# Streaming-window attention and an affine ResMLP on one core: the same tasks in another written-out order, with other engines and buffers

## The chip, the cores and the metric

The kernel runs on one core of one Trainium2 chip. The core has five engines, each with an instruction queue of its own that is worked through strictly in order: PE (TensorE, the matmul array), DVE (VectorE), ACT (ScalarE), POOL (GpSimd) and SP (SyncE, which here only issues DMAs). ACT and POOL can issue DMAs too. Engines wait for each other by semaphores; an instruction that waits holds up everything behind it on its engine.

The metric is the device time of one execution in microseconds (us), the median of several runs. One execution was profiled as well, and everything said of single instructions is from that one.

## The reference, cut to what matters

```python
# q, k, v: [4, 8, 768, 64]; n_sink 4, window 128
scores = scale * q @ k.transpose(0, 1, 3, 2)
keep   = (pos_k < n_sink) | ((0 <= pos_q - pos_k) & (pos_q - pos_k < window))
a      = softmax(where(keep, scores, -1e9))
x      = (a @ v)  as [4, 768, 512]

a1  = alpha1 * x + beta1
tok = einsum("ts,bsd->btd", w_tok, a1)        # w_tok: [768, 768]
u   = x + lam * tok
a2  = alpha2 * u + beta2
ch  = relu(a2 @ w_ch1) @ w_ch2                # 512 -> 2048 -> 512
out = u + lam * ch
```

## The kernel before

The four batches go one after another through the same stages, and the stages of neighbouring batches are interleaved. A row block is 128 of the 768 positions, so a batch has six; heads are taken in pairs, or in two groups (G) of four.

*Loading.* `load_qk` (L412) loads one pair of heads of q or k. For the pairs 1 to 3 of batch 0 POOL issues a DMA that casts to fp16 on the way; the rest come as fp32 on SP's or ACT's queue and are cast by an engine (`trans`, L505; the casts and copies are done in a helper and have its lines, L168 on ACT and L170 on DVE and POOL). `load_v0` (L441) loads v of batch 0, `load_wtok` (L458) w_tok, `load_w` (L468) a part of the second weight (512 KB, `wst_w`), `load_w1` (L474) the first weight by POOL. `gate` (L481) is a tiny DMA on SP that waits for a part of the first weight; loads behind it on SP start no sooner. Semaphores of a queue's DMAs are used in turn, eight of them, so a DMA waits for the landing of the one eight before it.

*Attention.* `trans` transposes q and k by matmuls with an identity (tp, L532 and L535) into a PSUM bank, and an engine copies them out (qkT). Scores are matmuls with qkT (S, L645, and L709 in `scores_by_pair`), ACT takes the exponential (E, L667, L714), masks are put on, and `pv` (L735) multiplies by v (cast to vfs) and divides by the sum.

*The ResMLP.* alpha1 and beta1 arrive as rows la_b and lb_b (`la1_b` and `lb1_b` in the code) in four partitions; `fold_rows` (L1317) multiplies them by lam (lam_r) and spreads them by a shuffle (L1319, L1321). In batch 0, xh is x times la_b. `cast_wtok` (L830) casts a row block of w_tok (wt, L842 or L844), transposes it (wT, L837) and copies it out (wtokT). `tok` (L868) multiplies wtokT and xh, and adds the result to x; u is cast, transposed (uTp, L921), and `mlp1` (L952) gives h, which ACT or DVE turns into hT (relu). `prod` (L1163) and `mlp2` (L1260) multiply by the second weight (P, ch).

*What sets the order.* All of this is written as some 1230 tasks, by `Plan.add`, which has nothing to say about when they run. Three tables do: `ORDER` lists the task numbers in the order in which their instructions are written into the queues; digit i of `ENGINES` is the engine of task i (0 to 4: ACT, DVE, PE, POOL, SP); `HOMES` gives the number of the buffer or PSUM bank that each buffer of a task lives in. `IDLES` names five tasks ahead of which dummy matmuls (`idle`, L161) are written to keep PE running, with the PSUM bank that they write and their count: 67 ahead of task 46 in bank 0, 25 ahead of task 90 in bank 1, and three smaller blocks. `emit` puts it together:

```python
for i in order:
    t = self.tasks[i]
    e = (ACT, DVE, PE, POOL, SP)[int(engines[i])]
    idle = fills.get(i)
    if idle:
        self.fill[1](self.pools["d"][0].tile(
            [128, 512], FP32, tag=f"d_{idle[0]}", bufs=1, name=f"idle{t.i}"), idle[1])
    ...
    t.fn(e)
```

Semaphores follow from that: an instruction waits for what it reads, and for the last user of the buffer that it writes.

Of the kernel before, what the change touches and what calls it, by code (L numbers as in the profile page):

```python
# [80 lines left out]
def kernel(  # L81
# [129 lines left out]
    for r in range(NR):  # L211
# [18 lines left out]
        6, 7, 0, 26, 1, 10, 5, 2, 9, 11, 45, 18, 8, 19, 48, 3, 22, 15, 46, 4, 49, 12,  # L230
        50, 14, 17, 47, 13, 16, 90, 43, 103, 39, 41, 91, 28, 72, 104, 95, 53, 54, 63,
        51, 42, 73, 52, 21, 44, 74, 20, 96, 109, 100, 40, 107, 110, 65, 24, 68, 108, 92,
        69, 55, 61, 56, 93, 97, 101, 98, 59, 30, 94, 102, 111, 23, 99, 62, 113, 57, 114,
        25, 112, 116, 60, 105, 115, 58, 27, 128, 64, 106, 117, 31, 131, 135, 29, 129,
        125, 132, 138, 66, 130, 179, 78, 126, 122, 178, 140, 118, 139, 123, 197, 127,
        136, 119, 137, 32, 70, 146, 120, 141, 133, 33, 84, 79, 134, 124, 144, 147, 80,
        85, 71, 150, 121, 86, 142, 75, 67, 154, 143, 151, 76, 148, 158, 155, 145, 152,
        77, 87, 166, 156, 159, 81, 162, 167, 160, 88, 163, 82, 168, 89, 213, 157, 164,
        34, 35, 83, 209, 153, 217, 149, 214, 218, 210, 229, 219, 211, 215, 212, 226,
        165, 216, 36, 230, 185, 220, 161, 177, 223, 222, 176, 232, 221, 224, 204, 225,  # L240
        175, 227, 257, 169, 237, 233, 279, 238, 199, 234, 171, 258, 273, 280, 231, 186,
        259, 228, 274, 182, 277, 172, 260, 241, 278, 174, 246, 200, 295, 170, 248, 247,
        291, 296, 37, 181, 187, 243, 293, 292, 242, 289, 198, 294, 384, 267, 188, 290,
        281, 268, 173, 271, 349, 282, 180, 285, 272, 358, 301, 351, 286, 378, 303, 189,
        203, 297, 302, 192, 304, 249, 366, 190, 379, 298, 250, 287, 369, 380, 385, 205,
        288, 283, 191, 375, 386, 367, 265, 284, 368, 352, 370, 363, 376, 266, 253, 381,
        377, 371, 299, 254, 372, 615, 364, 206, 300, 382, 201, 365, 373, 275, 374, 383,
        357, 261, 276, 183, 387, 408, 262, 614, 263, 409, 202, 269, 184, 411, 410, 395,
        264, 239, 621, 617, 412, 397, 240, 270, 388, 400, 396, 235, 616, 196, 244, 398,
        401, 255, 245, 236, 390, 256, 193, 359, 389, 251, 399, 207, 311, 195, 252, 391,  # L250
        424, 426, 393, 335, 392, 360, 425, 636, 312, 194, 427, 208, 336, 394, 648, 428,
        413, 634, 419, 414, 622, 404, 420, 337, 405, 429, 402, 415, 313, 422, 416, 421,
        361, 441, 305, 403, 442, 638, 423, 626, 406, 314, 640, 619, 437, 315, 430, 443,
        316, 435, 431, 641, 338, 436, 362, 618, 433, 306, 438, 649, 341, 317, 432, 407,
        444, 637, 644, 307, 345, 439, 339, 620, 318, 445, 434, 628, 635, 450, 642, 308,
        451, 340, 440, 452, 639, 446, 453, 417, 319, 447, 645, 323, 418, 320, 309, 448,
        643, 658, 321, 324, 623, 449, 322, 329, 625, 659, 454, 646, 325, 347, 647, 330,
        455, 343, 326, 344, 353, 355, 464, 456, 465, 348, 466, 460, 650, 457, 467, 327,
        458, 331, 629, 461, 459, 462, 653, 632, 651, 463, 656, 332, 654, 356, 472, 627,
        652, 333, 342, 310, 38, 655, 660, 624, 480, 473, 468, 469, 470, 474, 885, 665,  # L260
        471, 476, 481, 475, 482, 488, 477, 350, 483, 492, 489, 478, 630, 490, 657, 493,
        479, 514, 491, 516, 328, 515, 882, 663, 518, 880, 517, 879, 498, 666, 661, 664,
        502, 499, 354, 508, 519, 512, 346, 509, 662, 678, 513, 671, 484, 679, 676, 486,
        503, 504, 487, 485, 677, 506, 877, 672, 680, 548, 507, 526, 505, 549, 334, 674,
        631, 522, 527, 907, 546, 681, 523, 633, 903, 528, 547, 534, 878, 529, 890, 675,
# [12 lines left out]
        986, 773, 752, 913, 886, 761, 919, 774, 604, 767, 918, 598, 762, 763, 768, 777,
        764, 779, 920, 923, 780, 987, 988, 989, 990, 914, 991, 992, 993, 755, 915, 778,
        608, 756, 926, 930, 735, 609, 924, 927, 931, 925, 753, 736, 781, 737, 893, 928,  # L280
        775, 782, 738, 892, 929, 934, 754, 932, 769, 610, 935, 941, 770, 819, 776, 894,
        942, 939, 820, 821, 940, 937, 936, 823, 749, 822, 748, 945, 824, 938, 747, 827,
        933, 948, 950, 750, 943, 952, 951, 825, 953, 787, 828, 944, 807, 788, 797, 826,
        808, 949, 946, 829, 954, 798, 801, 830, 791, 802, 947, 956, 792, 783, 957, 994,
        995, 996, 997, 961, 789, 784, 962, 958, 963, 964, 955, 790, 785, 959, 811, 965,
        805, 812, 786, 795, 806, 960, 967, 796, 799, 793, 968, 970, 966, 972, 794, 813,
        969, 971, 815, 973, 814, 809, 800, 974, 816, 803, 810, 976, 804, 978, 837, 975,
        979, 977, 835, 838, 980, 841, 836, 818, 839, 843, 842, 840, 981, 845, 844, 998,
        846, 817, 1002, 832, 831, 1006, 999, 1003, 1000, 1014, 1007, 1004, 1001, 833,
        1008, 1018, 1005, 834, 1022, 1015, 1009, 1019, 1016, 847, 1020, 1023, 1017, 851,  # L290
        848, 1021, 850, 855, 1010, 1024, 1012, 1011, 862, 1025, 1013, 852, 849, 856,
        868, 854, 858, 1050, 859, 1051, 863, 857, 869, 1026, 864, 1034, 860, 1082, 1028,
        1027, 871, 861, 1029, 870, 1030, 865, 853, 1031, 874, 872, 1032, 866, 1035, 873,
        1066, 867, 875, 1052, 1054, 876, 1033, 1053, 1056, 1055, 1038, 1058, 1083, 1036,
        1039, 1057, 1037, 1040, 1063, 1059, 1042, 1041, 1064, 1067, 1084, 1060, 1047,
        1043, 1085, 1070, 1048, 1072, 1061, 1071, 1074, 1045, 1049, 1062, 1068, 1065,
        1044, 1073, 1046, 1069, 1086, 1088, 1075, 1087, 1079, 1090, 1098, 1076, 1080,
        1114, 1099, 1077, 1115, 1089, 1081, 1078, 1095, 1100, 1091, 1116, 1096, 1130,
        1092, 1117, 1093, 1101, 1131, 1102, 1104, 1094, 1097, 1103, 1118, 1106, 1132,
        1162, 1119, 1134, 1133, 1120, 1111, 1135, 1122, 1136, 1112, 1146, 1138, 1127,  # L300
        1164, 1147, 1105, 1121, 1107, 1113, 1152, 1143, 1123, 1154, 1150, 1128, 1137,
# [1181 lines left out]
```

## Time and profile before

| | us |
|---|---|
| median of 3 runs | 250.66 (250.23 to 251.75) |
| span of the profiled execution, first to last instruction | 248.4 |
| PE busy | 242.9 (98%) |
| DVE busy | 208.0 (84%) |
| ACT busy | 136.1 (55%) |
| POOL busy | 126.0 (51%) |

The page gives the profiled execution's span, and not its time by the clock of the runs; the median of the runs is 2.3 us above that span. Names in the profile have their buffer numbers left out (la_b, qkT, S). A row of a group or of a timeline reads: line, engine, operation, output and inputs, shapes, count; in a timeline the first two numbers are start and duration in us, and a bracket at the end is the idle time of the engine just before it, with what ended it. PEld is PE's weight load, which runs beside its matmuls.

### The profile page before, as it was taken

Reading aid. Unit: us, or ns where it says so; the run is one execution under the profiler, and the core shown is the slowest. Engines: PE = TensorE matmul, PEld = TensorE weight load, DVE = VectorE, ACT = ScalarE, POOL = GpSimd, SP = SyncE. Lnnn points to the kernel's source line nnn. Section 1 sums busy time; section 2 is a strip of 40 time slices with the busy share of each in tenths; the row PEclk is TensorE's granted clock in tenths of the full one; section 3 lists DMA queues with packets and bytes.
Section 4 is the critical chain, followed back from the end, with each engine's and each line's share of the span. In section 5 each row is a group of like instructions: output and inputs, shape, how many; then the busy total and the mean of one; then the engine's idle time right before and its main releaser. Section 6 shows DMA issues by size and latency. Waiting matters only on the chain.

```text
span 248.4 us, 5583 instructions
## 1 busy us (share of the span) xinstructions
PE 242.9 (98%) x2151; PEld 159.2 (64%) x2151; DVE 208.0 (84%) x437; ACT 136.1 (55%) x229; POOL 126.0 (51%) x139
## 2 busy tenths in 40 slices
PE   8899999999999999999999999999999999999994
PEld 8654645676555544565677577568668477667883
DVE  6797987677697896798789998979798999899873
ACT  2399935688987124687833353666771234766000
POOL 8808733968866647413874012053746036556060
PEclk9999999999999999999999999999999999999999
DMA  6999999999999998899469445611000055200114
GB/s 207 210 247 297 248 211 304 355 362 287 219 196 210 254 179 178 180 247 200 106 131 203 85 84 161 170 21 45 3 0 3 4 101 186 93 0 3 65 42 150
DMA packets 86562, 38.80 MB, mean 156 GB/s; under 512 B 73588, under 2 KB 81276, under 8 KB 86536
## 3 DMA queue, kind: packets, MB, share of 16 engines
q1 hardware_dynamic: 67408, 29.11, 50.3%
q10 hardware_dynamic: 15384, 6.06, 10.4%
q0 software_dynamic: 3744, 3.28, 8.2%
q8 instruction: 17, 0.28, 0.5%
q14 instruction: 9, 0.07, 0.1%
HBM read 29.91 MB, written 6.29 MB: 146 GB/s over the span
## 4 chain that ended last, share of the span: by engine, by line
PE 90%; ACT 4%; DVE 3%; issue 2%; DVEq 0%; ACTq 0%
PE h L960 24%; PE P L1199 22%; PE tok L880 12%; PE ch L1269 8%; PE hA L1041 4%; PE pv L746 4%; PE S L645 4%; PE idle L161 2%; PE hE L1041 2%; PE tp L535 1%; ACT wt L842 1%; ACT E L667 1%; PE hB L1041 1%; DVE qkT L170 1%; PE tp L532 1%
## 5 line engine op out<-in xcount | busy, mean ns | idle before, releaser
L960 PE MATMUL h<-uT,w1f 128*128 128x384 f16 x384 | 68.0, 326 | 0.1
L960 PEld LDWEIGHTS <-w1f 128*128 128x128 f16 x384 | 35.9, 98 | 24.0 <-issue 2.0
L1199 PEld LDWEIGHTS <-hT 128*128 128x128 f16 x408 | 39.4, 98 | 6.6 <-DVE hT L1142 0.3
L667 ACT ACTIVATE E<-S 128x1024 f16<-128x1024 f32 (+1 forms) x39 | 38.0, 1002 | 7.0 <-PE S L645 5.4
L966 ACT ACTIVATE hT<-h 128x384 f16<-128x384 f32 x58 | 27.9, 492 | 21.5 <-PE h L960 17.9
L790 POOL TENSOR_TENSOR tm<-x,la_b 128x512 f32<-128x512 f32 x18 | 24.7, 1371 | 21.9 <-DVE xh L793 12.0
L880 PE MATMUL tok<-xh,wtokT 128*128 128x512 f16 x144 | 32.8, 379 | 0.0
L968 DVE TENSOR_SCALAR hT<-h 128x384 f16<-128x384 f32 x38 | 20.4, 553 | 8.1 <-PE h L960 7.7
L168 ACT CAST u<-x 128x512 f16<-128x512 f32 x17 | 10.4, 618 | 29.2 <-DVE x L887 28.0
L1199 PE MATMUL P<-w2f,hT 128*128 128x256 f16 x216 | 26.4, 273 | 0.0
L1212 DVE TENSOR_TENSOR x<-x,P 128x256 f32<-128x256 f32 x45 | 18.0, 415 | 7.2 <-PE P L1199 6.9
L880 PEld LDWEIGHTS <-wtokT 128*128 128x128 f16 x144 | 13.8, 98 | 15.2 <-issue 0.2
L1199 PE MATMUL P<-w2s,hT 128*128 128x256 f16 x192 | 22.9, 273 | 0.0
L1269 PE MATMUL ch<-w2f,hT 128*128 128x512 f16 x96 | 22.7, 379 | 0.0
L772 DVE TENSOR_TENSOR x<-pv,rec 128x256 f32<-128x256 f32 x48 | 20.4, 425 | 1.7
L168 ACT CAST n<-nat 128x768 f16<-128x768 f32 x20 | 16.2, 830 | 8.1 <-DMA out_dram<-x 4.8
L746 PEld LDWEIGHTS <-E 128*128 128x128 f16 x328 | 15.2, 97 | 4.9 <-issue 1.1
L170 POOL CAST u<-x 128x512 f16<-128x512 f32 x7 | 4.6, 663 | 26.1 <-DVE x L887 16.9
L746 PE MATMUL pv<-vfs,E 128*128 128x65 f16 x328 | 17.7, 194 | 0.0
L887 DVE TENSOR_TENSOR x<-x,tok 128x512 f32<-128x512 f32 x24 | 15.9, 681 | 1.8 <-PE tok L880 1.5
L607 POOL TENSOR_SCALAR_AFFINE_SELECT E<-E 128x512 f16<-128x512 f16 x12 | 8.6, 740 | 16.9 <-ACT E L667 16.9
L170 POOL CAST vfs<-vnat 128x512 f16<-128x512 f32 x18 | 13.9, 778 | 5.1 <-PE pv L746 4.2
(161 smaller groups left out, 432.4 us busy)
## 6 DMA issues: line engine op xcount, KB each, us to landing
wst_w<-in_moe_w_ch_dram SPq DMA_DIRECT2D x8, 512.0 KB, 7.9
nat<-in_q_dram SPq DMA_DIRECT2D x10, 384.0 KB, 4.2
nat<-in_k_dram SPq DMA_DIRECT2D x10, 384.0 KB, 8.2
vnat<-in_v_dram SPq DMA_DIRECT2D x14, 256.0 KB, 6.2
out_dram<-x SPq DMA_DIRECT2D x11, 256.0 KB, 3.3
wtn<-in_moe_w_tok_dram SPq DMA_DIRECT2D x6, 384.0 KB, 4.4
w1f<-in_moe_w_ch_dram POOLq DMA_DIRECT2D x4, 512.0 KB, 10.6
out_dram<-x ACTq DMA_DIRECT2D x7, 256.0 KB, 4.5
```

The costliest lines, as they stand in the source:

```text
L168: nc.scalar.copy(o, i)
L170: engine[e].tensor_copy(o, i)
L667: nc.scalar.activation(eT.t, pS.t[:, :, 0 : n * w].rearrange("p e (i w) -> p e i w", i=n), AF.Exp, scale=scale)
L746: nc.tensor.matmul(po.t[:, hl, :], eT.t[:, e_, off + i, c : c + P], vf[j][:, h, :], start=(r < 2 and n == 0), stop=(n == len(parts) - 1 an ...
L772: nc.vector.tensor_mul(bx.t[:, 4 * G : 4 * G + 4, :], po.t[:, :, 0:D], rec.t.to_broadcast([P, 4, D]))
L790: engine[e].tensor_mul(bt.t, bx.t.rearrange("p h d -> p (h d)"), la1_b)
L880: nc.tensor.matmul(bank(), wtokT[:, si, ti * P : (ti + 1) * P], hs[si].t, start=(si == 0), stop=(si == NR - 1))
L960: nc.tensor.matmul(ph.t, w1f[:, c, fi * P : (fi + 1) * P], bu.t[:, c, chk * NTOK : (chk + 1) * NTOK], start=(c == 0), stop=(c == NC - 1))
L966: nc.scalar.activation(bh.t[:, fi, :], ph.t, AF.Relu)
L968: nc.vector.tensor_scalar_max(bh.t[:, fi, :], ph.t, 0.0)
L1199: nc.tensor.matmul(pc.t, hh[:, nt * P : (nt + 1) * P], w(fi), start=(first and n_ == 0), stop=(n_ == HF - 1), skip_group_check=True)
L1269: nc.tensor.matmul(pc.t, bh.t[:, fi, nt * P : (nt + 1) * P], w2f[:, fi, :], start=(fi == 0), stop=(fi == NF - 1))
```

## The change

The three tables `ORDER`, `ENGINES` and `HOMES` have other contents. The tasks, what each computes, the block sizes and `IDLES` are as before. The new tables are four lines shorter, so lines of the changed kernel are four less than those of the kernel before (L1319 becomes L1315). PE has the same instructions in another order; DVE has 415 entries in its queue in place of 407, ACT 245 in place of 251, POOL 136 and then 156, SP 117 and then 113.

```diff
     ORDER = (
-        6, 7, 0, 26, 1, 10, 5, 2, 9, 11, 45, 18, 8, 19, 48, 3, 22, 15, 46, 4, 49, 12,
...
+        6, 8, 1, 2, 7, 39, 40, 0, 10, 26, 45, 48, 46, 49, 50, 18, 9, 5, 12, 15, 16, 14, 47,
...
     ENGINES = (
-        "3313134433443333444444444444444433334443111211211212021212021203331121211210210200201210"
...
+        "3313134433443333444444444444444433334441111211201212120212120201330321211210200210201210"
     HOMES = (
-        "145602340010102001213310200221013302203140101100511203013044215120821000003331a501103130"
...
+        "614305260320123101330313122103022001311150041201301200110151313020840143310220a501133150"
...
     IDLES = (
         (46, 0, 67), (90, 1, 25), (109, 3, 2), (166, 1, 4), (162, 0, 1),
     )
```

In the rows below, numbers at the end of a name are those of the buffer (tp_0_1 is pair 0's k, tp_0_0 its q), and a bracket names the semaphores for which an instruction waits: DMAHW4 in DVE's rows is the landing of lam_r, DMAHW6 that of la_b, DMAHW1 and DMAHW3 those of q and k of pair 0.

DVE, at the start of the program. Before:

```order
L376 TENSOR_SCALAR biasn<-maskn 128x256 [waits DVE_49]
L170 CAST n_0_0_0_143<-nat_0_0_113 128x2x6x64 [waits DMAHW1_49]
L170 CAST n_0_0_1_149<-nat_0_1_115 128x2x6x64 [waits DMAHW3_49]
L406 COPY vs<-bm 128x8 [waits Pool_49]
L170 COPY qkT_242<-tp_0_1_233 128x768 [waits PE_49]
L170 COPY qkT_242<-tp_0_0_225 128x768
L1319 TENSOR_TENSOR lb_b<-lb_b,lam_r 128x512 [waits DMAHW4_49,DMAHW0_49,DVE_49]
L844 TENSOR_SCALAR wt_0_292,rsum<-wtn_121 128x768 [waits DMAHW5_49,DVE_49]
L170 COPY qkT_242<-tp_1_1_299 128x768 [waits PE_49]
```

And DVE after the change:

```order
L372 TENSOR_SCALAR biasn<-maskn 128x256 [waits DVE_49]
L1315 TENSOR_TENSOR la_b<-la_b,lam_r 128x512 [waits DMAHW6_49,DMAHW4_49,DVE_49]
L1317 STREAM_SHUFFLE la_b<-la_b 128x512 [waits DVE_49]
L170 CAST n_0_0_0_138<-nat_0_0_113 128x2x6x64 [waits DMAHW1_49]
L170 CAST n_0_0_1_140<-nat_0_1_126 128x2x6x64 [waits DMAHW3_49]
L170 COPY qkT_224<-tp_0_1_217 128x768 [waits PE_49]
L170 COPY qkT_224<-tp_1_0_281 128x768 [waits PE_49]
L840 TENSOR_SCALAR wt_0_315,rsum<-wtn_136 128x768 [waits DMAHW7_49,DVE_49]
```

The product and shuffle of la_b, which were on POOL and later on DVE, now stand ahead of the casts of the first q and k. The copy of tp_0_0 has gone to ACT, where it is the first instruction with data. lb_b's product and the cast of wt_0 no longer stand ahead of pair 1's copy.

PE, at the end of the first transposes, where the 25 dummy matmuls begin (one row of each kind). Before:

```order
L535 MATMUL tp_0_1_233<-iden,n_0_0_1_149 128x128
L161 LDWEIGHTS warm
L161 MATMUL idle_251<-warm 128x128
...
L709 LDWEIGHTS qkT_242 [waits DVE_49]
L709 MATMUL S_0_0_0_277<-qkT_242 128x256 [waits DVE_49]
```

And PE after the change:

```order
L531 MATMUL tp_0_1_217<-iden,n_0_0_1_140 128x128
L161 LDWEIGHTS warm
L161 MATMUL idle_243<-warm 128x128 [waits Activation_49]
...
L705 LDWEIGHTS qkT_224 [waits DVE_49]
L705 MATMUL S_0_0_0_269<-qkT_224 128x256
```

tp_0_0 now lives in the bank that the dummies write, so the first of them waits for ACT's copy of it.

PE, between the last pv of batch 0 and its tok (a row or two of each kind). Before:

```order
L739 MATMUL pv_4_1_728<-vs,es_426 128x260 [waits PE_49]
...
L746 MATMUL pv_4_1_728<-vfs,E_4_1_673 128x65
L837 MATMUL wT_742<-iden,wt_5_703 128x128 [waits DVE_49]
...
L837 MATMUL wT_752<-iden,wt_3_724 128x128 [waits PE_49]
...
L880 MATMUL tok_1_761<-xh_0_478,wtokT 128x512 [waits Pool_49]
...
L880 MATMUL tok_0_771<-xh_0_478,wtokT 128x512 [waits Activation_49]
```

And PE after the change:

```order
L735 MATMUL pv_4_1_732<-vs,es_393 128x260 [waits PE_49]
...
L742 MATMUL pv_4_1_732<-vfs,E_4_1_679 128x65
L876 MATMUL tok_0_744<-xh_0_526,wtokT 128x512 [waits Pool_49]
...
L876 MATMUL tok_1_754<-xh_3_569,wtokT 128x512
L833 MATMUL wT_761<-iden,wt_5_759 128x128 [waits DVE_49]
...
L833 MATMUL wT_771<-iden,wt_3_707 128x128 [waits PE_49]
```

Eight tok matmuls now stand ahead of the last two transposes of w_tok.

Elsewhere: on POOL, the load of q of pair 1 is now the very first instruction after the start, and the load of q of pair 3 waits for DVE's first cast, whose source buffer it takes. ACT has one cast of v (768 wide) that DVE had, and DVE three of the xh products that POOL had. On SP, before, the weight w_0, the row lam_b and the weight w_12 went ahead of the gate; now the load of k of pair 3 of the next batch does, and w_4, lam_b and w_12 come behind it. w_0 and w_6 are now issued on ACT, between two of its hT evictions, and wait there for loads of k and q of the next batch to land.

More of the change, by code (lines that the diff above doesn't have):

```diff
@@ L229 @@
     ORDER = (
[79 rows of a table removed]
[75 rows of a table added]
     )
     ENGINES = (
-        "3313134433443333444444444444444433334443111211211212021212021203331121211210210200201210"
-        "2020201202011202020202020213213213213213213202002020202020213121312131213121312131444444"
-        "4444413114433334413314413314444042210221021021020121321021321202020020211212020202020212"
-        "1212020212120202120212020212121202020202022221022221422221022221422221022221013111111331"
-        "1311333333302002002132132002132002102020101212010321213120301212131201012121312010121213"
@@ L316 @@
-        "1203212131212131213421342104011121042104213400012120202021202021212120202020212120202121"
-        "2121202111202021202120202011202121212121111121212121212121132111213121421021421421421044"
-        "4400004440443333330404040404040404020201012120101212133201012121312030121213120101212133"
-        "2032121312121312104210421040001210421042104000121212120212020212121202120202021202121202"
-        "0202020112020202020212020112021212121211111212121212121213121112131214214214210214214044"
@@ L321 @@
-        "4404404404433333304040404043404040202010121203012121312010121213320103212131203012121312"
-        "0321213321213111111111111111112104210421040011210421342134010111332021202201120211202120"
-        "2211320211202121220132121320202022013202112021212201120213202020220112021320202122013202"
-        "11202020220132021111112020210202142141111212121212121211302133021314210214210214210214"
+        "3313134433443333444444444444444433334441111211201212120212120201330321211210200210201210"
+        "2020201202010202020202020213213213213213211202012020202020213121312131211121112131444444"
@@ new lines @@
+        "4440411314033334413114411134000042210221021321121021321021321202120020200212021202021212"
+        "1202120202121212020212020212121212121202022221022221422221422221022221022221411131131113"
+        "1331333333332032032032132002002002102020101212010121213120103212131203012121312010121213"
+        "3201212131212131210421042104101121342104213401102120212021202021212021202020212021202021"
+        "2121202111212021202120202111202021212121111121212121212121132111213121421021021421421444"
@@ new lines @@
+        "4440440404443333330404040404040404020201012120301212131201032121332010121213120103212133"
+        "2032121312121312104213421040000213421042104000020202020202120202120212020202120212120202"
+        "0202021112020202020202020112120212121211111212121212121213321112133214214214214210214444"
+        "0440440404433333304043434340404041202010121203012121332010321213320101212133203012121312"
+        "0321213321213313331133331113112134210421340000213421342104000131132120212211120213202120"
@@ L325 @@
+        "2201121211202120220132121120202022013202112121202201321211202121220132021120202122011202"
+        "11202020220112021111112020210202142101111212121212121211102113421310214210214210210210"
     )
     HOMES = (
-        "145602340010102001213310200221013302203140101100511203013044215120821000003331a501103130"
-        "5140011112031102051467032311003221123033120133001001032002203212113003320023113113103113"
-        "20311022642130030020210001112300123101450093004101001b3002014531200000131101000502017200"
@@ L330 @@
-        "3206010112033310021331123331330302113210001232150012232123130221212022310345033723010320"
-        "103100135301020081002011411421050103321a003101204000011011051003031104020013001303110312"
-        "0021102210121102223200511310123320031102132301035337572302312010320101420152002210101311"
-        "162103012154110041003020b005101119102307200010323002312203102012310101300213420235320230"
-        "01141123522003311247002301135231000210"
+        "614305260320123101330313122103022001311150041201301200110151313020840143310220a501133150"
@@ new lines @@
+        "0110411012031001043250744311230020323213220130031221132101230300120302003233123111123123"
+        "0331102221642000012013230123310102501043019000501103070104104331600030112002110105001310"
+        "021b310200012133321101032333302032201111301233175132232100032213201111303205704131030230"
+        "0213001103103201a10050154114110310031203002012150150011103080040101100010331231302221302"
+        "1300230110201000223227311312123320130023301130773505333020311023010101220130109200301122"
@@ L335 @@
+        "1220051012300b10010305417001110201104306210210233103012322321013203143301200131034212251"
+        "22140033022115304223012003175203311201"
     )
```

152 rows, old and new, of the table ORDER are left out of this document.

## The prediction

> **What bounds the kernel now.** I read the page's totals first, then a table of stretches, then the timelines of single engines in the stretches that are not full, and the chain of waits.
>
> ```profile
> PE 242.9 (98%) x2151; PEld 159.2 (64%) x2151; DVE 208.0 (84%) x437; ACT 136.1 (55%) x229; POOL 126.0 (51%) x139
> ```
>
> PE is busy for 98% of a span of 248.4 us (242.9 over 0.98, the time from first to last instruction). The stretches say where the rest lies (length, then busy time and count of PE, PEld, DVE, ACT, POOL, granted clock, DMA share, GB/s):
>
> ```profile
> 0.00:10.00 10.00, 8.29 (x108) 7.92 (x109) 6.43 (x24) 1.41 (x2) 9.25 (x23) 1.00 0.91 209
> 10.00:20.00 10.00, 9.66 (x148) 5.36 (x149) 9.38 (x23) 8.62 (x16) 2.93 (x4) 1.00 1.17 237
> 20.00:30.00 10.00, 9.76 (x137) 5.62 (x136) 8.65 (x26) 9.92 (x17) 8.03 (x12) 1.00 1.01 277
> 30.00:245.00 215.00, 214.94 (x1765) 140.32 (x1765) 183.15 (x366) 116.20 (x197) 105.76 (x102) 1.00 0.65 145
> ```
>
> From 30 to 245 us PE is busy 214.94 of 215. The change leaves every PE instruction as it was, so nothing can be won there; a bubble can only be added. What PE can lose or win lies in the head, where DVE (first 20 us) and ACT (9.92 of 10 in the third stretch) take turns as the bound. I therefore walk the head by hand, old and new order side by side, and look at the rest only for stalls. The span is 248.4; the median of the runs is 250.66, which is 2.3 above it, and I carry that difference over.
>
> The head of before, PE, DVE and then ACT (start, duration, what, and in brackets the idle time ahead):
>
> ```profile
> 6.81 0.83 PE L535 MATMUL tp<-iden,n 128*128 128x128 f16 x12
> 7.48 1.56 PE L161 MATMUL idle<-warm 128*128 128x128 f16 x25
> 9.55 0.29 PE L709 MATMUL S<-qkT 64*128 64x256 f16 x2 [0.52 <-DVE qkT L170]
> ```
> ```profile
> 3.96 0.71 DVE L170 CAST n<-nat 128x768 f16<-128x768 f32 x1 [0.23 <-DMA nat<-in_q_dram]
> 4.97 0.56 DVE L170 CAST n<-nat 128x768 f16<-128x768 f32 x1 [0.29 <-DMA nat<-in_k_dram]
> 5.91 0.18 DVE L406 COPY vs<-bm 128x8 f16<-128x8 f16 x1 [0.38 <-POOL bm L386]
> 7.68 1.82 DVE L170 COPY qkT<-tp 128x768 f16<-128x768 f16 x2 [1.59 <-PE tp L535]
> 9.42 1.14 DVE L1319 TENSOR_TENSOR lb_b<-lb_b,lam_r 128x512 f32<-128x512 f32 x1
> 10.48 0.94 DVE L844 TENSOR_SCALAR_CACHE_REDUCE wt<-wtn 128x768 f16<-128x768 f32 x1
> ...
> 13.75 0.73 DVE L1321 STREAM_SHUFFLE la_b<-la_b 128x512 f32<-128x512 f32 x1
> ```
> ```profile
> 2.31 0.61 ACTq L205 DMA_DIRECT2D lam_r<-in_moe_lam_dram  x1
> 2.96 0.51 ACTq L205 DMA_DIRECT2D la_b<-in_moe_alpha_dram  x1
> ...
> 11.64 0.80 ACT L168 COPY qkT<-tp 128x768 f16<-128x768 f16 x1 [0.47 <-PE tp L532]
> 12.34 0.60 ACT L714 ACTIVATE E<-S 128x512 f16<-128x512 f32 x1
> 13.42 1.94 ACT L667 ACTIVATE E<-S 128x1024 f16<-128x1024 f32 x2 [0.47 <-PE S L645]
> ```
>
> So q and k are cast by 5.53, transposed from 6.81 (PE fills with dummy matmuls till then), and the first score matmul starts at 9.55.
>
> **The change, part by part.**
>
> *Step 1, la_b's product ahead of the first casts.* On DVE the product and shuffle of la_b now stand ahead of the casts of the first q and k, and wait for lam_r and la_b. When those land shows in SP's queue, where loads wait for the landing of earlier ones; the first row below waited for lam_r, the third, two loads on, for la_b:
>
> ```profile
> SPq L452 <- DMA lam_r<-in_moe_lam_dram: 1.4, 1, 1.4
> ```
> ```profile
> 6.94 0.37 SPq L452 DMA_DIRECT2D v<-in_v_dram  x1
> ```
> ```profile
> 8.12 1.16 SPq L452 DMA_DIRECT2D v<-in_v_dram  x1
> ```
>
> lam_r landed just before 6.94, la_b by 8.12; la_b was issued 0.65 later than lam_r, so I take 7.4 (bounds 6.94 and 8.12). A product of this size alone on DVE is 0.69, and it was 1.14 beside POOL's (rows below and above):
>
> ```profile
> 33.53 0.69 DVE L887 TENSOR_TENSOR x<-x,tok 128x512 f32<-128x512 f32 x1 [0.61 <-PE tok L880]
> ```
>
> 7.4 + 0.69 + 0.73 (shuffle) = 8.8; the two casts end at 9.5 and 10.1, and the transposes begin at 9.5 in place of 6.81: +2.7 (bounds +2.2 and +3.9).
>
> *Step 2, two eviction engines and a block of dummies that waits.* The two qkT copies ran in series on DVE (1.82); now ACT takes the first (0.80) and DVE the second (0.94): −0.9. But the 25 dummies between transposes and scores now write the bank which that ACT copy reads, and wait for it: the second set of transposes ends near 10.7, the ACT copy near 10.8, the block (1.4 to 1.56) near 12.25, 0.8 to 0.9 behind the DVE copy that was ready: +0.9. The first score starts near 12.25 instead of 9.55, +2.7 up to here.
>
> *Step 3, lb_b's product and the first w_tok cast behind pair 1.* In before the next eviction waited on DVE behind 1.14 + 0.94 (9.42 to 11.42). That DVE queue is now shorter, so the first full E comes at about 15.4 instead of 13.42: −0.7, +2.0 in all (bounds 0 and −2.1 for the step).
>
> *Step 4, a vfs cast on ACT, in the stretch where ACT is full.* In that stretch:
>
> ```profile
> 19.86 1.02 ACT L667 ACTIVATE E<-S 128x1024 f16<-128x1024 f32 x1 [0.33 <-PE S L645]
> ...
> 26.74 1.52 ACT L667 ACTIVATE E<-S 128x1024 f16<-128x1024 f32 x2
> ```
> ```profile
> L168 ACT CAST n<-nat 128x768 f16<-128x768 f32 x20 | 16.2, 830 | 8.1 <-DMA out_dram<-x 4.8
> ```
>
> A 128x768 cast on ACT is 830 ns; 0.33 of idle soaks up part: +0.5 (0 to +0.83). But the two last E's, the rows of 26.74, change places, so that the short one (1.52 less a full one's 0.9) is no longer behind: −0.6. DVE, which loses two such casts, was not the bound here and gives nothing. The last E ends near 30.15 instead of 28.26, +1.9.
>
> *Step 5, eight tok matmuls ahead of the last two wT.* Before, the wait there was:
>
> ```profile
> 29.23 0.50 PE L837 MATMUL wT<-iden,wt 128*128 128x128 f16 x6
> 29.96 0.51 PE L837 MATMUL wT<-iden,wt 128*128 128x128 f16 x6 [0.24 <-ACT wt L842]
> 30.31 6.64 PE L880 MATMUL tok<-xh,wtokT 128*128 128x512 f16 x30
> ...
> 38.81 4.28 PE L960 MATMUL h<-uT,w1f 128*128 128x384 f16 x24
> ```
>
> Eight of the tok matmuls (6.64/30 each, 1.8) cover ACT's last casts: −0.3 (the 0.24 and its restart). The tok inputs are ready by then. h begins at 40.4 instead of 38.81: +1.6.
>
> *Step 6, q(1,0) first on POOL's queue.* This load now precedes lam_r and la_b, and competes with them and with k(0,1). At the 209 GB/s of the first stretch its 384 KB are 1.9 us if everything waits for it, nothing if the queues share. I take +0.3, nearer to sharing, since lam_r, a few KB, landed in 4 us under three loads of that size (bounds 0 and +1.9).
>
> *Step 7, loads moved to ACT later.* w_0 and w_6 are now issued on ACT between two hT evictions, and wait for the landing of earlier loads, k and q of the next batch:
>
> ```profile
> nat<-in_k_dram SPq DMA_DIRECT2D x10, 384.0 KB, 8.2
> ```
> ```profile
> 38.06 0.40 SPq L425 DMA_DIRECT2D nat<-in_k_dram  x1
> ```
> ```profile
> 43.76 7.87 PE h L960 x48
> ```
>
> In the new order the gate, two weights and lam_b stand ahead of these on SP, so with the +1.6 I put their issue at 41 to 42, and their landing 8.2 later near 50. The run of h matmuls that ended the chain at 51.63 would end at 53.2, the last of them in banks that DVE empties; I estimate that ACT is missed from 51.7 on. I take +0.4 (0 to +3). Other loads and gates that move are issued well ahead of use under the 215 us in which PE has work queued: 0 (a gate's own issue would be under 1).
>
> *Step 8, small moves on POOL and DVE.* POOL's q(3,0) load waits for DVE's first cast, now at 9.5, and vfs casts wait behind it; POOL works only 2.93 of the second 10 us, so this fits: 0, and up to +1 if a pv is then short of its vfs. Three xh products go from POOL to DVE, in a stretch with 1.35 idle there, for under 0.5 each: 0 (up to +0.5). The tail's P matmuls stand in the same order on PE: 0.
>
> Sum: 2.7 − 0.9 + 0.9 − 0.7 + 0.5 − 0.6 − 0.3 + 0.3 + 0.4 = +2.3. Span 248.4 + 2.3 = 250.7; with the 2.3 around it **253.0 us**; the forecast's own range is 251.8 to 254.0.
>
> **The rivals.** *The clock falls back.* At the start the same dummy ran at two speeds, while the granted clock reads 1.00 in both (stretches of the dummies alone; length, PE busy, PEld busy, clock, DMA):
>
> ```profile
> 1.10:4.60 3.50, 3.50 (x34) 3.50 (x35) 1.00 0.85 242
> 4.80:6.40 1.60, 1.60 (x33) 1.60 (x31) 1.00 0.95 285
> ```
>
> 103 ns each for the first 3.5 us, then 48. In the new order PE sits idle from 6.66 to 9.5, 2.84 us. If such a gap returns it to the slow pitch, the 25 dummies cost 25 × 55 ns = 1.4, and another 2 us of transposes and scores run at up to double time, about 0.4 of it on the path: 253.0 + 1.8 = 254.8. Against it: no gap in before is that long, so no row shows a fall. It decides from the gap's length. The Trainium skill's page "TensorE: Matmul & The Clock Gate" (Part 1, "What's actually happening") says that the default is half the clock and that one idle window of about 3.4 us, in a free-running count, brings it back; by that rule the start's slow 3.5 us agrees, and 2.84 us is short of a whole window, so by it the time stays 253.0, unless step 1 comes out near its upper bound and stretches the gap past 3.4; then it is 254.8.
>
> *ACT stalls on its DMA issues.* If k and q land later than 51.7, ACT's hT evictions stand behind the issue, h banks fill and PE stops: landing 10 us after issue instead of 8.2 gives some 2 us: 253.0 − 0.4 + 2.4 = 255.0. For it: in before most such waits sit on SP, where nothing hangs behind them. Against: the median landing leaves 1.7 us.
>
> *The other side: la_b lands early.* If lam_r and la_b land by 5, where SP's queue shows only a bound set by its own order of waits, the product and shuffle (1.42) fit in before the dummies end at 6.66. Then steps 1 and 6 vanish, and the block's wait is ACT's copy only (8.5 + 1.4 = 9.9, +0.35): 0.35 − 0.7 + 0.5 − 0.6 − 0.3 + 0.4 = −0.35, so 250.3, not slower. It decides at a landing of about 5.2; for it speaks only that a few KB need not take 4 us.
>
> **How the numbers follow.** Measurement can tell about 1%, 2.5 us: faster is under 248.2, slower over 253.2. Forecast 0.45: it lies just inside the bound, so 0.25 same and 0.20 slower. Clock 0.18: 0.15 slower, 0.03 same. ACT's stalls 0.17: 0.14 slower, 0.03 same. Early la_b 0.20: 0.12 same, and 0.08 faster, if steps 3 and 5 reach their low ends. Together 0.08, 0.43, 0.49. The range 250.0 to 256.2 takes in the forecast, half of the early case, and all but the worst of the two slow ones.
>
> **What would show it.** Right: on DVE la_b's product starts at 7.4 and the first cast at 8.8; the 25 dummies start near 10.85 behind ACT's copy, the first score near 12.25, h near 40.4; from there PE has no bubble over half a us. A pitch of 100 ns in the 25 dummies is the clock; an ACT wait over 5 us at w_0 or w_6 with PE idle is the second rival; a first cast before 6 is the third. The sum is wrong if the first score is late but h is not, for then the head has slack that I don't see.

## The result, and the profile after

The changed kernel takes 259.95 us (median of 4 runs, 259.8 to 261.05) against 250.66, a ratio of 1.0364 (95% interval 1.033 to 1.0399): slower by 3.6%, and above the forecast's range. The profiled execution's span is 258.3 us against 248.4. The page's first line and its clock slices:

```profile
PE 246.6 (95%) x2151; PEld 161.7 (63%) x2151; DVE 207.1 (80%) x431; ACT 134.3 (52%) x222; POOL 140.4 (54%) x154
...
PEclk9779999999999999999999999999999999999999
```

The same 2151 matmuls now take 246.6 us, 3.7 more, and in two of the 40 slices, near the start, the granted clock is below 9 tenths. The table of stretches, with the columns of the one shown of the kernel before:

```profile
0.00:10.00 10.00, 6.23 (x67) 6.06 (x67) 4.20 (x22) 1.28 (x1) 5.79 (x17) 0.97 0.85 201
10.00:20.00 10.00, 8.96 (x98) 6.44 (x98) 5.25 (x12) 4.98 (x9) 3.06 (x6) 0.69 1.12 225
20.00:30.00 10.00, 9.52 (x139) 5.16 (x137) 9.21 (x23) 9.61 (x15) 3.36 (x6) 1.00 0.61 210
30.00:255.00 225.00, 221.93 (x1855) 144.00 (x1851) 188.06 (x376) 118.44 (x198) 128.19 (x127) 1.00 0.65 142
```

Two things are to be seen: the second stretch has a clock of 0.69 (1.00 before) and 98 matmuls in place of 148; and from 30 us on PE stands idle for 3.07 us, where it had 0.06. A finer table of the same view says where:

```profile
30.00:60.00 30.00, 29.89 (x262) 18.36 (x259) 24.60 (x49) 19.58 (x34) 16.44 (x21) 1.00 1.02 263
60.00:90.00 30.00, 28.50 (x251) 15.66 (x249) 24.85 (x48) 22.17 (x32) 18.52 (x19) 1.00 1.19 229
90.00:185.00 95.00, 93.56 (x782) 59.52 (x781) 79.18 (x159) 49.30 (x80) 60.62 (x62) 1.00 0.72 144
```

For all kernels below I use three places that are the same piece of work in each: the first score matmul, the first h, and the last 160 P matmuls, by which PE ends. Of the changed kernel the first two are in PE's timeline, and the third in the chain of waits (the second row of the last pair is that of the kernel before):

```profile
15.03 0.39 PE L705 MATMUL S<-qkT 64*128 64x256 f16 x2
```
```profile
44.56 1.76 PE L956 MATMUL h<-uT,w1f 128*128 128x384 f16 x9
```
```profile
237.52 17.48 PE P L1195 x160
```
```profile
227.75 17.48 PE P L1199 x160
```

The first score is 5.5 late (9.55 before), the first h 5.75 (38.81), the end 9.8. So the loss has two parts: 5.8 us in the head, nearly all of it ahead of the first score, and 4.0 us behind the first h, where PE's idle time lies between 60 and 185 us. From the first h to the last P PE runs 1554 matmuls in both kernels; 2.9 of the 4.0 us are idle time, and the other 1.1 stand as longer busy time of as many matmuls, which no run here explains.

*The head.* DVE's and PE's timelines, and the clock (the table of stretches again, with PE's columns alone):

```profile
8.62 0.69 DVE L1315 TENSOR_TENSOR la_b<-la_b,lam_r 128x512 f32<-128x512 f32 x1 [4.48 <-DMA la_b<-in_moe_alpha_dram]
...
9.97 1.01 DVE L170 CAST n<-nat 128x768 f16<-128x768 f32 x2
```
```profile
1.05 6.23 PE L161 MATMUL idle<-warm 128*128 128x128 f16 x67 [1.05 <-DVE warm L187]
10.57 1.46 PE L531 MATMUL tp<-iden,n 128*128 128x128 f16 x12 [3.29 <-DVE n L170]
12.28 2.83 PE L161 MATMUL idle<-warm 128*128 128x128 f16 x25 [0.25 <-ACT qkT L168]
```
```profile
8.00:9.00 1.00, 0.00 (x0) 1.00 1.15 223
9.00:10.00 1.00, 0.00 (x0) 0.68 1.27 238
10.00:11.00 1.00, 0.43 (x5) 0.50 1.30 217
...
15.00:16.00 1.00, 1.00 (x14) 0.50 1.30 226
16.00:17.00 1.00, 1.00 (x23) 0.90 1.28 233
```

DVE waits 4.48 us for la_b, PE 3.29 for DVE's casts, and in that gap the clock goes to 0.50; it comes back near 16.2. The transposes take 1.46 (0.83 before), the 25 dummies 2.83 (1.56).

*From 60 to 185 us.* PE's waits, summed by what ended them (total, times, longest); the kernel before has the second row, and else none over the 0.52 ahead of its first score:

```profile
PE tp L531 <- DVE n L170: 3.3, 1, 3.3
PE idle L161 <- DVE warm L187: 1.0, 1, 1.0
PE pv L742 <- POOL vfs L170: 0.7, 1, 0.7
PE h L956 <- DVE x L768: 0.6, 1, 0.6
PE pv L735 <- DVE x L1276: 0.6, 1, 0.6
PE P L1195 <- ACT pt L168: 0.5, 1, 0.5
```

Each of the last four has a place of its own. POOL's cast of v waited for its load, which ACT issued at 64.06 (row block 1) and, once that buffer was free, at 73.25 (row block 3) (in the kernel before, row block 1's was issued on SP at 39, the third row):

```profile
64.06 0.38 ACTq L431 DMA_DIRECT2D vnat<-in_v_dram  x1
```
```profile
73.25 0.37 ACTq L431 DMA_DIRECT2D vnat<-in_v_dram  x1
```
```profile
39.02 0.46 SPq L435 DMA_DIRECT2D vnat<-in_v_dram  x1
```
```profile
72.61 0.61 POOL L170 CAST vfs<-vnat 128x512 f16<-128x512 f32 x1 [3.90 <-DMA vnat<-in_v_dram]
...
79.97 0.61 POOL L170 CAST vfs<-vnat 128x512 f16<-128x512 f32 x1 [4.66 <-DMA vnat<-in_v_dram]
```

That holds PE up at 72.6 (pv), and behind the second cast, by way of POOL's products for xh and DVE's additions, at 84:

```profile
83.02 1.07 DVE L789 TENSOR_TENSOR xh<-tm,lb_b 128x512 f16<-128x512 f32 x1 [0.73 <-POOL tm L786]
84.01 0.68 DVE L1276 TENSOR_TENSOR x<-x,ch 128x512 f32<-128x512 f32 x1
```

At 112 us a division of pv stands on DVE behind two sums of the second weight, and at 179 a copy of P stands on ACT behind a uT that waits for a DMA transpose (DVE, then ACT):

```profile
111.25 1.60 DVE L1110 TENSOR_TENSOR w2f<-w2f 128x512 f16<-128x512 f16 x2
112.77 0.17 DVE L767 RECIPROCAL rec<-pv 128x4 f32<-128x4 f32 x1
```
```profile
178.96 0.71 ACT L900 ACTIVATE uT<-uT,ab 128x384 f16<-128x384 f16 x1 [0.94 <-DMA uT<-u]
179.57 0.35 ACT L168 COPY pt<-P 128x256 f32<-128x256 f32 x1
```

### The profile page after: what moved, and what is told of

Read it like the earlier page. It is cut to its first block, busy times and chain, and to the rows that moved or that the text cites. A ratio compares the mean times of both kernels' runs of the same rounds, so it can differ in the third digit from the quotient of the medians.

```text
span 258.3 us, 5585 instructions
## 1 busy us (share of the span) xinstructions
PE 246.6 (95%) x2151; PEld 161.7 (63%) x2151; DVE 207.1 (80%) x431; ACT 134.3 (52%) x222; POOL 140.4 (54%) x154
## 5 line engine op out<-in xcount | busy, mean ns | idle before, releaser
L956 PE MATMUL h<-uT,w1f 128*128 128x384 f16 x384 | 68.9, 326 | 0.6 <-DVE x L768 0.6
L962 ACT ACTIVATE hT<-h 128x384 f16<-128x384 f32 x55 | 26.5, 492 | 19.8 <-PE h L956 18.7
L964 DVE TENSOR_SCALAR hT<-h 128x384 f16<-128x384 f32 x41 | 22.6, 554 | 9.7 <-PE h L956 8.8
L168 ACT CAST u<-x 128x512 f16<-128x512 f32 x13 | 8.0, 617 | 33.0 <-DVE x L883 32.1
L170 POOL CAST u<-x 128x512 f16<-128x512 f32 x11 | 7.8, 710 | 24.4 <-DVE x L883 13.8
L883 DVE TENSOR_TENSOR x<-x,tok 128x512 f32<-128x512 f32 x24 | 16.2, 684 | 2.7 <-PE tok L876 2.3
L678 DVE TENSOR_TENSOR E<-E,maskn 128x1024 f16<-128x1024 f16 x16 | 13.5, 859 | 3.1 <-ACT E L663 3.1
L900 ACT ACTIVATE uT<-uT,ab 128x384 f16<-128x384 f16 x18 | 11.6, 699 | 6.9 <-DMA uT<-u 3.7
```

What stands on the lines that cost most here:

```text
L170: engine[e].tensor_copy(o, i)
L883: nc.vector.tensor_add(xf, xf, bank())
L956: nc.tensor.matmul(ph.t, w1f[:, c, fi * P : (fi + 1) * P], bu.t[:, c, chk * NTOK : (chk + 1) * NTOK], start=(c == 0), stop=(c == NC - 1))
L962: nc.scalar.activation(bh.t[:, fi, :], ph.t, AF.Relu)
L964: nc.vector.tensor_scalar_max(bh.t[:, fi, :], ph.t, 0.0)
```

## The experiments

Theory: the head's loss is la_b's product ahead of the first casts, with the clock that falls in the gap; the later loss has causes of its own. All runs are in this table; ratios are to the kernel before on the same chip, the last three columns are the three places in the profiled execution.

| run | median us | ratio (95%) | first score | first h | last 160 P |
|---|---|---|---|---|---|
| before | 250.66 | | 9.55 | 38.81 | 227.75 |
| changed | 259.95 | 1.0364 (1.033 to 1.0399) | 15.03 | 44.56 | 237.52 |
| e1_la_back | 254.93 | 1.0156 (1.0121 to 1.0191) | 9.89 | 40.05 | 232.91 |
| e2_la_first (on before) | 253.16 | 1.0091 (1.0063 to 1.0118) | 12.37 | 41.57 | 230.56 |
| e3_warm | 257.65 | 1.0256 (1.0229 to 1.0282) | 13.74 | 43.22 | 235.55 |
| e4_v1_early | 259.47 | 1.0321 (1.0275 to 1.0367) | 14.71 | 43.82 | 235.04 |
| e5_q10_back | 257.31 | 1.0257 (1.0236 to 1.0279) | 12.71 | 42.63 | 235.48 |
| e6_la_v1 | 256.11 | 1.021 (1.0179 to 1.0241) | 10.23 | 39.34 | 232.89 |
| e7_la_v1_sums | 253.74 | 1.0131 (1.0111 to 1.0151) | 9.09 | 39.57 | 229.91 |
| e8_before_two (on before) | 250.91 | 1.001 (0.9988 to 1.0032) | 8.67 | 38.25 | 227.98 |
| e9_w_back | 255.39 | 1.018 (1.0118 to 1.0242) | 10.19 | 40.11 | 234.79 |
| e10_w_q10_back | 256.21 | 1.0197 (1.017 to 1.0225) | 9.53 | 40.00 | 233.62 |
| e11_la_q10_first (on before) | 256.01 | 1.0193 (1.0173 to 1.0213) | 15.68 | 44.99 | 233.87 |
| e12b_v1_late (on before) | 251.38 | 1.0013 (1.0 to 1.0026) | 9.18 | 39.03 | 228.29 |
| e13_la_sums_pt | 253.61 | 1.0103 (1.0085 to 1.0121) | 9.16 | 39.70 | 230.77 |
| e15_v1_mid | 252.27 | 1.0057 (1.0036 to 1.0079) | 10.12 | 39.60 | 229.63 |
| e16_k11_first | 252.92 | 1.0067 (1.0047 to 1.0088) | 9.83 | 39.92 | 231.01 |

The edits move tasks in ORDER, ahead of the call of `emit`, by this helper (39 and 40 are la_b's product and shuffle, 50 the first qkT copy on DVE, 2 the mask biases):

```diff
+    order, engines, idles = list(ORDER), list(ENGINES), IDLES
+    def move(ids, behind):
+        for i in ids:
+            order.remove(i)
+        k = order.index(behind) + 1
+        order[k:k] = ids
+    move([39, 40], 50)                                        # e1
-    plan.emit(ORDER, ENGINES, HOMES, IDLES)
+    plan.emit(order, engines, HOMES, idles)
```

**e1_la_back.** 

> The changed kernel with la_b's product and shuffle put back behind the first two casts and the first qkT copy on DVE; nothing else differs. Theory: the 5.6 us by which PE is behind after 20 us come from that product's wait (lam_r and la_b landed at 8.6) and from the slow clock that follows the idle stretch; without it the casts start near 4, the first score near 10, the granted clock is never 0.50, and PE is at most 1 us behind at 20 us. The later losses (4.1 us between 69 and 185 us) have causes of their own and stay: 254 to 256 us. Rival one: the later losses only follow the head's delay and go too: 250.5 to 252. Rival two: the head is late for another reason: over 258.

By the medians 5.0 us of the 9.3 went, and the clock was 1.00 throughout; the later loss stayed (192.9 us from the first h to the last P, against 188.9 before and 193.0 in the changed kernel), though PE came to it 4.5 us earlier. Theory held; the first rival (the later loss follows the head) fell. The first h is still 1.2 late (40.05 against 38.81).

**e2_la_first.** The kernel before with `move([39, 40], 2)` and `engines[39] = "1"`.

> The kernel before with one thing of the change: la_b's product and shuffle on DVE ahead of the first casts (the product was on POOL). Theory: the wait alone makes most of the head's loss. With la_b landing at 7.4 PE stands idle some 2.8 us and the clock stays: 253 to 254.5. With la_b at 8.6, as in the changed kernel, the idle stretch is over 3 us, the clock falls to 0.50 and it is 255.5 to 257. Rival: PE's dummies and DVE's slack hide the wait: 250 to 251.5.

+2.1 us by the medians (251.06 for the kernel before on that chip), 2.3 by the ratio. DVE's timeline of this run has the step as it was forecast, to a tenth; PE's row of the first transposes stands under it:

```profile
7.53 0.69 DVE L1319 TENSOR_TENSOR la_b<-la_b,lam_r 128x512 f32<-128x512 f32 x1 [3.79 <-DMA la_b<-in_moe_alpha_dram]
...
8.88 1.01 DVE L170 CAST n<-nat 128x768 f16<-128x768 f32 x2
```

```profile
9.48 0.98 PE L535 MATMUL tp<-iden,n 128*128 128x128 f16 x12 [1.73 <-DVE n L170]
```

The time is in the theory's first range. PE stood idle for 1.73 us and not 2.8, because its first dummies took longer in this execution (6.70 us), and the clock stayed at 1.00. In the other three executions the mean granted clock was 1.00, 1.00 and 0.993, the last of them with 254.12 us in place of 252.95 to 253.19, so there it seems to have fallen. The product alone is not the changed kernel's loss: there la_b came 1.1 later.

**e3_warm.** The changed kernel with `idles = ((46, 0, 132),) + IDLES[1:]`.

> The changed kernel with 132 dummy matmuls in place of 67 ahead of the first transposes, so that PE runs until the casts are done and has no idle stretch of over 3 us; la_b's product still stands first. Theory: the clock stays at 1.00 after its start, the 25 dummies take 1.4 and not 2.8, the transposes 0.8 and not 1.5, and 2.0 to 2.6 us are won: 257.4 to 258. Rival: what the slow clock cost would have been waiting anyway (evictions, E): 259.3 to 260.

2.3 us won and a clock of 1.00: theory, the slow clock's share, with la_b's wait left as it was (the product begins at 8.90). In the profiled execution 1.3 of them are won by the first score and 2.0 by the last P.

**e4_v1_early.** The changed kernel with `move([204], 197)` and `engines[204] = "4"` (204 loads v of batch 1, row block 1; 197 is w_12's load).

> The changed kernel with one load moved: v of batch 1, row block 1, issued on SP behind the weight w_12 (near 40 us) and not on ACT at 64. Theory: POOL's casts of v waited for it (3.9 us) and, through the buffer that it holds, for row block 3's load (4.7 us), and PE lost 2.0 us at 72 to 84; that goes: 257.7 to 258.2, and the rest of the difference stays. Rival one: another wait takes the place, and 0 to 0.7 us are won: 259.2 to 260. Rival two: the earlier load collides with the second weight's loads: over 260.2.

Inconclusive by time: the four runs spread from 257.5 to 260.1. In the profiled one, the fastest of them (its slow clock lasts 3.4 us, the changed kernel's 6.8), h to the last P took 191.2 us against the changed kernel's 193.0.

**e5_q10_back.** The changed kernel with `move([8], 9)`: POOL's load of q of pair 1 behind that of k.

> The changed kernel with one load moved on POOL: q of pair 1 behind the masks and behind k of pair 1, as in the kernel before; la_b's product still stands ahead of the first casts. Theory: that early load is what made lam_r and la_b land at 8.1 and 8.6, where the run of the kernel before with only the product moved had 7.1 and 7.5. Without it the product starts near 7.5, PE's idle stretch ahead of the first transposes shrinks from 3.3 to about 2, the clock doesn't fall, and 2.5 to 3.5 us are won: 256.4 to 257.4. Rival one: the landing is set by the queues' other order (v ahead of w_tok) and stays at 8.6: 259.5 to 260.3. Rival two: la_b lands earlier but the clock falls all the same: 258.5 to 259.

2.6 us less than the changed kernel's 259.95, as the theory had it, but not wholly for its reason. The product began at 7.02 in place of 8.62 and the first score came 2.3 earlier, but in the profiled execution the clock still fell, later than PE's gap of 2.61 us (6.35 to 8.96) and while PE was at work again:

```profile
8.96 0.97 PE L531 MATMUL tp<-iden,n 128*128 128x128 f16 x12 [2.61 <-DVE n L170]
```
```profile
9.00:10.00 1.00, 0.94 (x12) 1.00 1.24 233
10.00:11.00 1.00, 0.64 (x11) 0.92 1.27 232
11.00:12.00 1.00, 1.00 (x12) 0.50 1.29 199
```

It did not fall each time: the mean granted clock is 0.993 in the two executions of 257.84 us and 0.999 in those of 256.52 and 256.79. So without that load the clock's fall is a matter of the execution, and where it doesn't fall 3.2 to 3.4 us are won.

**e11_la_q10_first.** The kernel before with e2's edit and `move([8], 6)`: the two suspects of the head together, nothing else.

> The kernel before with two things of the change: la_b's product and shuffle on DVE ahead of the first casts, and q of pair 1 as POOL's first load. With the product alone the kernel before lost 2.1 us, and the clock stayed. Theory: the load makes lam_r and la_b land some 1.1 later (8.6), PE's idle stretch grows from 1.7 to about 2.8, the clock falls to 0.50, and the two together cost 4 to 5.5 us: 255 to 256.5. Rival: the two only add up, 1.1 more and the clock stays: 254 to 254.4.

256.01: theory. The head's loss is there in full (first h 44.99, the changed kernel 44.56), and no more of it: from h to the last P it takes 188.88 us against 188.94 before. The load cost more than the 1.1 expected: the product began 2.1 later than in e2 (7.53), and PE's gap was 4.39 us. DVE's row and PE's:

```profile
9.67 0.69 DVE L1319 TENSOR_TENSOR la_b<-la_b,lam_r 128x512 f32<-128x512 f32 x1 [4.84 <-DMA la_b<-in_moe_alpha_dram]
```
```profile
11.62 1.46 PE L535 MATMUL tp<-iden,n 128*128 128x128 f16 x12 [4.39 <-DVE n L170]
12.87 2.87 PE L161 MATMUL idle<-warm 128*128 128x128 f16 x25
```

**e8_before_two.** The kernel before with `engines[47] = "0"` (tp_0_0's copy on ACT) and 16 dummies for 25.

> The kernel before with the one part of the change that was costed as a gain in the head: the copy of tp_0_0 on ACT beside DVE's of tp_0_1, and 16 dummies in place of 25 behind the first transposes, so that they end with the copies. Theory: the first score starts 0.6 to 0.9 earlier and all behind it follows: 249.9 to 250.4 if before has 251.0. Rival: ACT's E and the later copies are the bound, and nothing is won: 250.8 to 251.2.

Rival: the first score came 0.9 earlier and the first h 0.6, and nothing of it is left at the end. PE, early, waited for two loads of later pairs and for a cast instead (three waits of 0.2 to 0.3 that the kernel before doesn't have).

**e6_la_v1, e7_la_v1_sums, e9_w_back, e10_w_q10_back.** e1's edit with e4's; then `move([350, 346], 505)` (two sums of the second weight behind DVE's work of 112 us); then `move([179, 186], 204)` on SP (w_0 and w_6); then e5's edit.

> The run with la_b's product put back (254.9), and v of batch 1, row block 1, loaded on SP near 40 us as well. With the clock at 1.00 throughout, the load's effect can be measured without the scatter of the slow clock. Theory: 1.6 to 2.1 us of the later loss go: 252.8 to 253.4. Rival: other waits take their place: 254.4 to 255.2.

> The run before this one with one more step: on DVE, two sums of the second weight (L1110) that stand ahead of a division of batch 2 near 112 us are put behind it. Theory: PE's wait of 0.8 us for that division goes, and nothing else: 0.8 under the run before it. Rival: the next bubble grows: no difference.

> The changed kernel with la_b's product put back, v of batch 1's row block 1 loaded early on SP, the two sums behind the division, and now the weights w_0 and w_6 too on SP, behind that v load, and no more on ACT. Theory: in the run with la_b and v put back, w_0 and w_6 were issued by ACT at 47.5 and 48.1, after ACT had waited for q of the next batch to land; they landed at 54.6, DVE's scaling of them held up its hT behind it, and PE lost 1.9 us there. Early on SP that wait can't happen: 250.9 to 252.2, and the runs scatter less than the 2.5 us that they did. Rival: the loads behind them (k and q of the next batch) are late instead, and nothing is won or it is worse: 253.5 to 255.5.

> The run before this one, and q of pair 1 loaded on POOL behind the masks and k of pair 1. Theory: PE waited 1.0 to 1.4 us near 10 us for k of pair 1 in two of the runs with la_b's product put back, since k's load came late behind the masks; with k first that wait goes, but q comes later: 0 to 0.8 us under the run before it. Rival: the head's bound is DVE and ACT, no difference.

In e6 the rival held, and more: 256.11, over its range and e1's 254.93. v no longer waited, but PE's longest wait was a new one, hT on DVE, which stood behind the scaling of w_0 and w_6 that landed late. Moved early too (e9), they made k and q of the next batch late: PE waited for an hT on ACT behind a cast of them, and in the profiled execution the clock fell to 0.50 behind that gap of 2.26 us, for 3.4 us. One row of PE's waits from each, e6 and e9:

```profile
PE h L956 <- DVE hT L964: 1.7, 1, 1.7
```
```profile
PE tp L531 <- ACT hT L962: 2.3, 1, 2.3
```

e7's 253.74 is 2.4 under e6, not 0.8. The wait on DVE's hT is absent from its profiled execution, the fastest of the four (252.28), but whether it is absent from the others isn't shown. e10's expectation failed as well (256.21 against e9's 255.39: k came, q was late by 1.4). Between 35 and 55 us the DMA share is 1.07 in the changed kernel, and each load that was put ahead there (e6, e9) left another one late.

**e12b_v1_late.** The kernel before with `move([204], 387)`, `move([358], 360)` and `engines[204] = "0"`. In it two of the pv of batch 1 that use row block 1 precede its cast (358) in the order, and so multiply by the earlier batch's v and don't wait for the load.

> The kernel before with one thing of the change: v of batch 1, row block 1, loaded on ACT behind the copies of ks (near 59 us) and no more on SP at 39, and POOL's cast of it behind that of row block 3. Theory: PE waits for that cast near 67 us, as the changed kernel did at 72, and loses 0.7 to 2 us there: 251.7 to 253. Rival: the load lands in time, and the freed place on SP lets others land earlier: 250.4 to 251.4.

No difference, and it tells nothing on the wait, which it left out.

**e13_la_sums_pt.** e1's edit, `move([350, 346], 505)` and, on ACT, `move([747], 822)` (a uT behind the copy of P).

> The run with la_b's product put back (254.9), and two steps of order on engines, no load moved: on DVE the two sums of the second weight behind the division of batch 2 (the changed kernel's bubble of 0.8 us at 112 us), and on ACT a uT behind a copy of P (its bubble of 0.7 us at 179 us, where ACT waited for a DMA transpose with the copy queued behind). Theory: both bubbles go and nothing takes their place: 1.3 to 1.6 us under that run, 253.3 to 253.7. Rival: PE waits for the same tasks' successors instead: 254.4 to 255.2.

1.3 under e1, theory; the runs spread by 0.9 only. From 90 to 185 us PE is full again (93.56 in the changed kernel), and what is left lies in the stretch before:

```profile
60.00:90.00 30.00, 28.60 (x243) 14.87 (x238) 23.99 (x48) 18.81 (x24) 17.75 (x20) 1.00 1.23 235
90.00:185.00 95.00, 94.97 (x805) 61.26 (x804) 78.24 (x161) 53.26 (x86) 62.65 (x63) 1.00 0.66 131
```

**e15_v1_mid, e16_k11_first.** e13's edits with `move([204], 203)` on SP, behind v of row block 0; then `move([9], 8)`, k of pair 1 ahead of the masks on POOL.

> The run before (la_b's product, the two sums and the copy of P put back: 253.6), and v of batch 1, row block 1, issued on SP behind that of row block 0 near 51 us, when the loads of k, q, w_0 and w_6 have been issued, and not on ACT near 59. Theory: the 2.1 us that PE loses between 67 and 79 us come from this load alone; issued 8 us earlier, but behind the crowded stretch, it takes no other load's place, and they go: 251.4 to 251.9. Rival: as when it was issued near 37, another load is late in its place: 253.2 to 255.

> The run before this one, and POOL's load of k of pair 1 right behind that of q, ahead of the masks. Theory: the 1.0 to 1.5 us that PE waits for it near 10 us go, and 0.5 to 1.3 of them are left at 20 us: 250.3 to 251.2, as fast as the kernel before or a little faster. Rival: the masks, then the first casts or q and k of pair 0, are later by as much, and nothing is won: 251.4 to 252.

e15 came out between the two: 252.27, some 1.2 under e13 by their ratios. PE's wait for POOL's cast at 67 us is gone, and that for DVE's addition at 78 halved (0.3 for 0.6). From the first h to the last P it takes 190.0 us, where e13 took 191.1 and the kernel before 188.9: the late load of v is thus the cause of about half of the 2.1 us that e13 had left there. What is left of the wait at 78 is no longer the load's: POOL's second cast now waits for DVE. The rest, and its scatter (251.0 to 254.0), I can't assign. e16 won nothing (252.92, over its rival's range too): the wait for k of pair 1 is gone, and new ones of 0.39 stand at 19 and 51 us.

No version beat the kernel before.

## Why the prediction was wrong

- **Direction and mechanism of the head: right.** DVE's first cast waited behind la_b's product, the dummies waited for ACT's copy (0.25 us), and the first score was late by that and by the slow clock.
- **The sum, part by part, against the profile.** To the first transposes (steps 1 and 6) +3.0 was forecast, and it was +3.8 (10.57 against 6.81); from there to the first score (step 2) 0, and +1.7; to the first h (steps 3 to 5) −1.1, and +0.3; from there to the last P (step 7) +0.4, and +4.0. Together that is +2.3 and +9.8.
- **Step 6 is the term that failed first.** It gave q(1,0) on POOL +0.3, "nearer to sharing", within bounds up to 1.9. It cost 1.6 in the changed kernel (the product began at 8.62 with that load ahead, at 7.02 without, e5) and 2.1 on the kernel before (9.67 in e11, 7.53 in e2). Step 1's own numbers (7.4, 8.8) were those of e2.
- **The clock was a rival at 0.18 and belonged in the sum.** The condition that kept it out was too wide: the forecast gap of 2.84 us counted as safe up to 3.4, but in a gap of 3.29 the clock fell at about 9.4, 2.1 us after PE's last dummy (7.28). Its price of 1.8 was near: e3 got 2.3 back. The late load and the fall of the clock were taken as independent mishaps, while the first brings on the second. e2 and e11 show how steep that is: 2.1 us with the late product, 5.0 with the load added.
- **Steps 3 to 5: the gains didn't come.** From first score to first h they were to shorten 29.26 us by 1.1; the changed kernel took 29.53, and 29.48 with the clock at 1.00 (e3). Why is open for the three; e8 shows a like case for a gain of step 2's kind: engines that are done sooner met loads that weren't.
- **Step 7 priced the wrong load.** I took +0.4 for w_0 and w_6 on ACT and nothing for "other loads and gates that move". In the changed kernel w_0 and w_6 cost nothing that its profile shows; v of batch 1, moved from 39 us on SP to 64 on ACT, cost 1.0 to 1.2 us (e15 against e13). "Issued well ahead of use" does not hold for it: it was issued 4.7 us before POOL came to its cast (68.7) and took 8.5 to land, and row block 3's load waited for its buffer.
- **From 30 us on the forecast priced waits on DMAs, and not the order on DVE and ACT.** Two places, with waits of PE of 0.6 at 112 us and 0.5 at 179, cost 1.3 together (e13). PE's wait of 0.25 for DVE near 150 us is left open; no run tried it.
- **The other rivals.** la_b did not land early (8.6 and not 5). ACT's stall at w_0 and w_6 is not in the changed kernel; e6 shows its like, by DVE, when one more load stands ahead.

The account, by the ratios (3.64% of 250.66 is 9.1 us): 5.2 for la_b's product with the clock's fall (e1), 1.3 for the order on DVE and ACT (e13), 1.2 for v (e15), and 1.4 left over the kernel before, of which 0.8 stands at the first h in the profiles (39.60 against 38.81) and whose cause is open.

## What to carry to other kernels

When two edits act on the same wait, price them together at their upper bounds before calling a threshold out of reach: here a load of 384 KB and a product, each near 2 us, made a gap that cost another 2.3. For a moved load follow its buffer: who waits for it, when it comes free, and which load is issued into it next. Between 35 and 55 us, at a DMA share of 1.07, a load moved forward was a load moved back elsewhere (e6, e9), so in such a stretch compare whole orders and not single moves.

## What the hardware showed that I had not expected

The clock fell after gaps shorter than the 3.4 us that I had gone by: 2.26 us (e9), 2.61 (e5) and 3.29 (the changed kernel) brought it to 0.50, 1.73 (e2) and 1.75 (e6) did not. The Trainium skill's page "TensorE: Matmul & The Clock Gate" (Part 1, "What's actually happening") puts one idle window near 3.4 us, in a free-running count; the count's phase may be why e5's clock fell only when PE had been at work again for 2 us, but the runs show that a gap of less than a whole window is enough. The slow stretches agree with the window's length: by the slices of 1 us they are 3.4 us long in e4, e5 and e9, and 6.8, twice that, in the changed kernel and in e11. In the 3.4 us ahead of the fall PE had been idle for 2.1 us (the changed kernel), 2.0 (e5 and e11), 2.3 (e9) and all 3.4 (e4), estimates from the starts and durations of PE's rows; what share is needed, no run settles. The clock came back near 16.2 us in the changed kernel, 5.6 us after PE restarted.

The same 67 first dummies took between 5.2 us (e4) and 6.7 (e2) from one execution to the next, though PE's instructions up to there are the same; the start of the transposes moves with them. A single profile of this head is thus good to about 1 us, and the medians, not the profiled runs, carry the differences of that size.
